# Two neighbouring tokens per partition in a gated linear attention with an MLP mixer behind it, on one core

## The chip, the cores and the metric

The kernel runs on one core of a Trainium2 chip. A core has five engines with queues of their own that meet only at semaphores: TensorE (PE, matrix products into the eight banks of PSUM), VectorE (DVE), ScalarE (ACT), GpSimd (POOL) and SyncE (SP, which here only issues transfers). Transfers run on sixteen DMA engines that all queues share. PE loads the stationary operand (PEld) apart from the product itself. The metric is the time of one execution on the device in microseconds (us), lower is better.

## What is computed

Inputs are q, k, v and f_logit, each [4 batches, 8 heads, 768 tokens, 48], and four weight matrices. Per batch and head:

```python
f = 1.0 / (1.0 + np.exp(-f_logit))
for t in range(S):
    state = f[:, :, t, :, None] * state + np.einsum('bhd,bhe->bhde', k[:, :, t], v[:, :, t])
    y[:, :, t] = np.einsum('bhd,bhde->bhe', q[:, :, t], state)
```

The heads of y are put side by side (x is [4, 768, 384]), and a mixer follows, over the tokens and then over the channels:

```python
h = np.maximum(xt @ w_tok1, 0.0) @ w_tok2          # xt: x with tokens last; 768 -> 256 -> 768
u = x + h.transpose(0, 2, 1)
out = u + np.maximum(u @ w_ch1, 0.0) @ w_ch2       # 384 -> 1536 -> 384
```

## The kernel before, in words

**The attention in chunks.** 768 tokens are six chunks of 128. Within a chunk, a running sum L of log(1 + exp(-f_logit)) over the tokens turns the gates into factors: q is multiplied by exp(-L), k by exp(+L); then y is a masked product of scores within the chunk, plus q times the state that the chunks before left. A token is a partition: `load` (lines 351 to 363) brings one chunk of q, k, v (cast to bf16 on the way, on POOL's queue) or f_logit as 1024 runs of 192 bytes.

Per batch b and chunk c, on the engines:

- `gates` (443): ACT Exp and Ln of f_logit (450, 452), DVE or POOL the low part of the split into two bf16 halves (457).
- `sums_and_turns` (504): the running sums as two bf16 products with a triangle of ones, 384 columns each (530, 531; in batch 0 also 1-column products for the chunk's totals, 528 and 529, and two chunks in one fp32 product, 519); ACT takes exp of both signs (541, 543) and, from batch 1 on, the last rows (550), one partition of which SP spreads over the partitions (556, `glast`); DVE multiplies q and k by the factors (562); eight PE transposes (579) and copies to SBUF (592, or 430 and 432). In batch 3 SP's DMA transposes do that (569).
- `attention` (461): scores in eight products of 48 rows by 128 columns, two heads in the two halves of PE's rows (476); the chunk's part of the state in eight products whose 64 output columns go to the two halves of PE's columns (492). All other products use the whole 128x128 array.
- `rest` (597): DVE masks the scores into `AmT` (616), state and its bf16 copy `state_bd` are brought up to date (625 to 640), and the outputs are four products with the state (651) and eight with the masked scores (658), copied to x_nat (fp32) and x_bf (bf16).

Batches 1 to 3 take two chunks at a time.

**The mixer** (688): tok1 is 12 products of 384 columns (693), tok2 another 12 (709), both per batch; u is turned by PE (750) in batches 0 and 1 and by SP's DMA transposes (739) in 2 and 3; ch1 is 72 products (768), with a ReLU on ACT (439) or DVE (441) into zT; ch2 is 72 products (787), DVE adds u (793) and SP stores 128 token rows of 1536 bytes (797).

**The order of the work.** Nothing is scheduled by the hardware: `Plan.best` (176) walks the long list ORDER of operation numbers (and of the engine, where an operation may go to several), gives each a time from a table of costs (SLOTS and HELD are assumed landing times of batch 0's loads) and emits all in that order; the five queues then run in order and wait at semaphores. Where PE would idle early on, `idle` (832) issues products of a constant tile (834, `steady`). In batch 0 loads arrive chunk by chunk, the two token weights behind them; the loads of later batches run ahead.

Of the kernel before, what the change touches and what calls it, by code (L numbers as in the profile page):

```python
# [20 lines left out]
TURNED = 3  # L21
ORDER = (
# [60 lines left out]
)  # L83
KEPT = 3
SPLIT = 5
SLOTS = (5110, 5800, 7500, 8450, 9600, 10400, 11400, 13000, 14400, 14800, 16700,
         18000, 19100, 19500, 20000, 20700, 21400, 23400, 24300, 25900)
HELD = (2600, 3600, 4100, 4750, 5500, 6500)


class Op:
# [162 lines left out]
def kernel(  # L254
# [140 lines left out]
    for c in range(1, NCH):  # L395
        load("kq", 0, c)
        if c + 2 < NCH:
            mark(c + 2)
            load("f", 0, c + 2, SP)
# [468 lines left out]
```

## Time and profile before

| what | value |
|---|---|
| time, two runs | 173.04 and 174.04 us, median 173.54 |
| profiled execution, first to last instruction (its span) | 170.2 us; its time beyond that is not on the page |
| PE busy | 162.9 us, 96% |
| DVE, ACT, POOL busy | 128.0, 108.2, 99.3 us |
| matmuls in the program | 1605 |
| DMA packets | 102547, of which 95264 under 512 bytes |

The page of a profile gives, for each engine, its busy time; the span in 40 slices with the busy share in tenths; the DMA queues; the chain of work that ended last, followed back; and groups of instructions by line (L768 is line 768) and form. A group's busy time counts an instant once where instructions overlap; its mean is one instruction's own latency, which for pipelined products is longer than their spacing. The spacing is read from the starts in the timeline.

### The profile page before, as it was taken

The page shows a single profiled execution, that of the slowest core. Times are in us where ns is not written, and L with a number is a line of the kernel's source. Part 1 is how long each engine was busy: PE and PEld are TensorE (multiplying, and loading weights), DVE is VectorE, ACT ScalarE, POOL GpSimd, SP SyncE. Part 2 cuts the span into 40 slices and gives each one's busy share as a digit, 9 for nine tenths or more (in the row PEclk, how much of TensorE's full clock was granted, in tenths as well). Part 3 has the DMA queues.
Part 4 walks back from the last instruction along what each step waited for, and adds up shares of the span by engine and source line. Part 5 has one row for each costly group of instructions (what it writes and reads, how often), then busy time and mean ns, then how long its engine had stood idle before and what let it go on. Part 6 is the DMA issues. An engine that isn't in the chain of part 4 may idle for free.

```text
span 170.2 us, 4181 instructions
## 1 busy us (share of the span) xinstructions
PE 162.9 (96%) x1606; PEld 102.8 (60%) x1606; DVE 128.0 (75%) x287; ACT 108.2 (64%) x256; POOL 99.3 (58%) x134
## 2 busy tenths in 40 slices
PE   6899999999999999999999999999999999999992
PEld 2356565665766576665776756665666666566661
DVE  5679995966898998899999868768884723675431
ACT  4759993598879889999999978385545320510100
POOL 7999569896499969999978869603111200000000
PEclk9999999999999999999999999999999999999999
DMA  6999999999999997999998999996920060220253
GB/s 103 141 174 149 156 192 181 212 149 201 192 167 136 161 165 75 116 155 133 182 157 49 134 251 107 144 165 115 228 100 4 0 139 0 92 96 0 78 202 139
DMA packets 102547, 22.71 MB, mean 133 GB/s; under 512 B 95264, under 2 KB 101664, under 8 KB 102528
## 3 DMA queue, kind: packets, MB, share of 16 engines
q0 software_dynamic: 79440, 13.77, 101.8%
q1 hardware_dynamic: 22560, 8.59, 22.5%
q8 instruction: 12, 0.20, 0.5%
q10 hardware_dynamic: 528, 0.10, 0.3%
q14 instruction: 7, 0.06, 0.1%
HBM read 25.17 MB, written 4.72 MB: 176 GB/s over the span
## 4 chain that ended last, share of the span: by engine, by line
PE 64%; DMA 12%; DVE 7%; ACT 6%; POOL 6%; issue 2%; SPq 1%; DVEq 0%; POOLq 0%
PE ps L768 22%; PE ps L787 22%; DMA v_sb<-in_v_dram 5%; PE ps L709 4%; POOL qk_sb L360 4%; PE ps L693 4%; DMA glast<-ends 4%; DMA out_dram<-x_nat 3%; DVE AmT L616 2%; PE ps L476 2%; PE ps L579 2%; PE ps L658 2%; POOL v_sb L360 1%; PE ps L530 1%; PE ps L651 1%
## 5 line engine op out<-in xcount | busy, mean ns | idle before, releaser
L787 PE MATMUL ps<-w_ch,zT 128*128 128x384 bf16 (+2 forms) x300 | 51.6, 320 | 0.0
L768 PE MATMUL ps<-uT,w_ch 128*128 128x384 bf16 x288 | 50.6, 326 | 0.0
L439 ACT ACTIVATE zT<-ps 128x384 bf16<-128x384 f32 x56 | 25.3, 494 | 25.3 <-PE ps L768 25.2
L768 PEld LDWEIGHTS <-w_ch 128*128 128x128 bf16 x288 | 27.7, 98 | 17.7
L787 PEld LDWEIGHTS <-zT 128*128 128x128 bf16 x300 | 27.9, 98 | 16.9
L616 DVE TENSOR_TENSOR AmT<-ps,tri_bf 128x512 bf16<-128x512 f32 x46 | 30.5, 686 | 2.5 <-PE ps L476 2.3
L441 DVE TENSOR_SCALAR zT<-ps 128x384 bf16<-128x384 f32 x40 | 21.1, 554 | 8.8 <-PE ps L768 8.8
L360 POOL DMA_DIRECT2D v_sb<-in_v_dram x24 | 22.2, 925 | 4.1 <-DMA w_ch<-in_moe_w_ch_dram 4.1
L360 POOL DMA_DIRECT2D qk_sb<-in_k_dram x24 | 22.4, 932 | 0.8 <-POOLq L852 0.8
L360 POOL DMA_DIRECT2D qk_sb<-in_q_dram x24 | 22.3, 930 | 0.0
L793 DVE TENSOR_TENSOR x_nat<-x_nat,ps 128x384 f32<-128x384 f32 (+2 forms) x25 | 13.3, 535 | 10.6 <-PE ps L787 10.2
L360 POOL DMA_DIRECT2D f_sb<-in_f_logit_dram x18 | 16.5, 943 | 0.2
L562 DVE TENSOR_TENSOR qk<-qk_sb,GG 128x768 bf16<-128x768 bf16 (+1 forms) x30 | 14.2, 475 | 2.1 <-ACT GG L543 1.0
L450 ACT ACTIVATE f_sb<-f_sb 128x384 f32<-128x384 f32 x24 | 12.5, 524 | 4.6 <-DMA f_sb<-in_f_logit_dram 4.4
L434 POOL CAST state_bd<-state 48x192 bf16<-48x192 f32 x13 | 4.5, 347 | 16.2 <-DVE state L633 14.6
L725 DVE TENSOR_TENSOR x_nat<-x_nat,ps 128x384 f32<-128x384 f32 x21 | 10.5, 550 | 3.4 <-PE ps L709 3.1
L834 PE MATMUL ps<-steady 128*128 128x512 bf16 x30 | 11.3, 483 | 1.7 <-DVE steady L375 1.7
L543 ACT ACTIVATE GG<-ps 128x384 bf16<-128x384 f32 x24 | 11.6, 489 | 2.0 <-PE ps L531 1.9
L541 ACT ACTIVATE GG<-ps 128x384 bf16<-128x384 f32 x24 | 11.7, 488 | 1.4 <-PE ps L531 1.2
L579 PE MATMUL ps<-ident,qk 128*128 128x128 bf16 x144 | 11.6, 224 | 0.0
L579 PEld LDWEIGHTS <-qk 128*128 128x128 bf16 x144 | 9.2, 100 | 2.7 <-DVE qk L562 0.7
L550 ACT ACTIVATE ends<-ps 32x384 f32<-32x384 f32 x15 | 7.0, 481 | 4.9 <-PE ps L531 4.7
(81 smaller groups left out, 234.1 us busy)
## 6 DMA issues: line engine op xcount, KB each, us to landing
out_dram<-x_nat SPq DMA_DIRECT2D x23, 192.0 KB, 3.1
f_sb<-in_f_logit_dram POOLq DMA_DIRECT2D x18, 192.0 KB, 5.4
qk_sb<-in_k_dram POOLq DMA_DIRECT2D x24, 96.0 KB, 5.1
qk_sb<-in_q_dram POOLq DMA_DIRECT2D x24, 96.0 KB, 4.9
v_sb<-in_v_dram POOLq DMA_DIRECT2D x24, 96.0 KB, 5.5
w_ch<-in_moe_w_ch_dram POOLq DMA_DIRECT2D x2, 576.0 KB, 7.5
w_ch<-in_moe_w_ch_dram POOLq DMA_DIRECT2D x1, 1152.0 KB, 10.6
f_sb<-in_f_logit_dram SPq DMA_DIRECT2D x5, 192.0 KB, 4.7
```

The source lines that it names most:

```text
L360: lambda eng=eng, into=into, of=of: eng.dma_start(out=into, in_=of),
L439: nc.scalar.activation(out_, in_, AF.Relu, bias=0.0, scale=1.0)
L441: nc.vector.tensor_scalar(out_, in_, 0.0, None, ALU.max)
L450: add(ACT, r, lambda: nc.scalar.activation(fb, fb, AF.Exp, bias=0.0, scale=-1.0), make=[key], kind=el, need=([("fb", c)] if c < 1 else []) ...
L541: add(ACT, r, lambda: nc.scalar.activation(G[i], sview(), AF.Exp, bias=0.0, scale=-1.0), make=[("G", i)], bank=p_s, kind=el)
L543: add(ACT, r, lambda: nc.scalar.activation(Gi[i], sview(), AF.Exp, bias=0.0, scale=1.0), make=[("Gi", i)], bank=p_s, kind=el)
L562: add(DVE, r, lambda n=n: nc.vector.tensor_tensor(qk[i4][:, n, :, 0:D], qk_sb[nb][:, n, :, c, :], GG[i][:, n], ALU.mult), need=[(x, nb, c) ...
L579: nc.tensor.transpose(to[:, o + hp, :], blk(src)[:, hp, :], ident)
L616: add(DVE, r, lambda half=half, made=made: nc.vector.tensor_tensor(half, made(), tb4, ALU.mult), need=["tri_bf"], make=[("AmT", i, p)], ba ...
L768: nc.tensor.matmul(banks[pm.at][:, 0:384], lhsT=w[:, kt, c0:c0 + 128], rhs=uT[:, th, :, kt, :], start=(kt == 0), stop=(kt == 2))
L787: nc.tensor.matmul(banks[pm.at][:, 0:n1 - n0], lhsT=zT[:, kt, tt * 128:(tt + 1) * 128], rhs=w_ch2[:, kt, n0:n1], start=(kt == 0), stop=(kt ...
L793: add(DVE, rank("ch2", tt), lambda un=un, pm=pm, n=n1 - n0: nc.vector.tensor_tensor(un, un, banks[pm.at][:, 0:n], ALU.add), make=[("x_nat" ...
```

## The change

One partition now holds two neighbouring tokens, and two chunks (256 tokens) are one unit: partition q of pair P holds tokens 2q and 2q+1 (index j), and the two chunks are the two halves of the partitions (index x, 64 partitions each). The loads bring 384-byte runs, 1024 of them, once per pair.

- Exp and Ln run on 768 elements at a time, with Ln in place. DVE (in batch 0 once POOL) adds the two tokens of a partition (`two`), takes a low part for batches 1 to 3 (`two_lo`), and the sums are over token pairs: two bf16 products per pair of chunks in place of four, one fp32 product in batch 0, with a triangle that is zero between the two halves. This gives the sum at each second token; the first token's is had by subtraction on DVE (`first`). ACT takes four exponentials per pair, two of them from `first`.
- The scores of a pair are 32 products of 48 rows, 64 output columns and 128 streamed columns, in the four quarters of PE's array; the state's parts 32 (16 for a lone chunk) with 64 rows, 64 output columns and 48 streamed ones, in batch 0 in two lots of 16; the products with the state 16 per pair, with 64 output columns each; those with the masked scores 32, with 64 rows each.
- In the mixer the output tile of a chunk has token 2i+j in partition 64j+i. So w_tok1 is loaded in two halves of 64 partitions, each tok2 product becomes two, one for each half of the output partitions, and the store of a tile writes through a pattern of 2 x 64 rows where it was 128 rows.
- ORDER, SLOTS, HELD and the ranks are new. In the program of after the ReLU into zT is on ACT 71 times and on DVE 25 (56 and 40 before), three of the q,k multiplications of batch 0 are on POOL, and of the 25 stores twelve stand beside the last 48 products of ch2, some of them of batches 1 and 2.

The diff, cut to its core:

```diff
-            into = dst[i][:, :, cs, :]
-            of = src[b].rearrange("h (c t) d -> t h c d", t=C)[:, :, cs, :]
+    def runs(src, b, P):
+        return src[b].rearrange("h (c q j) d -> q h c (j d)", q=C, j=2)[:, :, P, :]
...
+    for j in range(2):
+        add(POOL, 5.0, lambda j=j: nc.gpsimd.dma_start(
+            out=w_tok1[64 * j:64 * j + 64], in_=moe_w_tok1.rearrange("(kt i j) n -> j i kt n", i=64, j=2)[j]),
...
+        op.fn = lambda op=op: both(op, two[i][:, :, 0:D], fb[:, :, 0], fb[:, :, 1], ALU.add)
+        if b:
+            add(DVE, r, lambda: nc.vector.tensor_tensor(two_lo[i], two[i][:, :, 0:D], two_hi[i], ALU.subtract),
...
+            if b == 0:
+                nc.tensor.matmul(pm, lhsT=tri, rhs=two[i][:, :, 0:D], start=True, stop=True)
+            else:
+                nc.tensor.matmul(pm, lhsT=tri2, rhs=two_hi[i], start=True, stop=False)
+                nc.tensor.matmul(pm, lhsT=tri2, rhs=two_lo[i], start=False, stop=True)
...
+        add(DVE, r, lambda: nc.vector.tensor_tensor(first[i], sview(), fb[:, :, 1], ALU.subtract),
...
+        def scores(js):
             for hp in range(HP):
+                for x in range(2):
+                    for par in range(2):
+                        rows = slice(par * 64, par * 64 + D)
+                        nc.tensor.matmul(
+                            banks[p_a[js][par].at][half[x], hp * 128:(hp + 1) * 128].rearrange("p (j t) -> p j t", j=2),
+                            lhsT=qkT[s][rows, js, 4 + hp, half[x]], rhs=qkT[s][rows, :, hp, half[x]], start=True, stop=True)
...
+                            nc.tensor.matmul(dg(x)[par * 64:par * 64 + 64, hp, :], lhsT=qk[s][half[x], js, 1, h, :],
+                                             rhs=v_sb[nb][half[x], h, 2 * P + js, :],
...
+        def before(x, start):
             for hp in range(HP):
+                for j in range(2):
+                    nc.tensor.matmul(yh(x)[half[j], 2 * hp:2 * hp + 2, :], lhsT=qkT[s][:, j, hp, half[x]],
+                                     rhs=state_bd[(2 * P + x - 1) % 3][:, hp, :],
...
+                        nc.tensor.matmul(yh(x)[:, h, :], lhsT=AmT[i][half[x], js, (h % 2) * 4 + h // 2, :],
+                                         rhs=v_sb[nb][half[x], h, 2 * P + js, :],
...
-                    nc.tensor.matmul(banks[pm.at][:, 0:DM], lhsT=w_tok2[:, kt, tt * 128:(tt + 1) * 128],
+                    for j in range(2):
+                        nc.tensor.matmul(banks[pm.at][64 * j:64 * j + 64, 0:DM], lhsT=w_tok2[:, kt, tt * 128 + j:(tt + 1) * 128:2],
...
-        rows = out[b].rearrange("(tt p) n -> tt p n", p=128)
+        rows = out[b].rearrange("(tt i j) n -> tt j i n", i=64, j=2)
...
-                add(SP, rank("ch2", tt), lambda un=un, to=to: nc.sync.dma_start(out=to, in_=un),
-                    need=[("x_nat", xn, tt, n0) if end else ("x_nat", xn, tt)], kind=("fix", 350, 2000, 580))
+                add(SP, rank("ch2", tt), lambda un=un, to=to: store(to, un),
+                    need=[("x_nat", xn, tt, n0) if end else ("x_nat", xn, tt)], kind=("fix", 420, 4000 if b < 3 else 2000, 580, 0))
```

More of the change, by code (lines that the diff above doesn't have):

```diff
@@ L185, in best @@
         ports: dict = {DVE: [], POOL: []}
+        turned: list = []
         done = []
@@ L375 @@
     nc.vector.memset(steady, 1.0)
-    load_half(0, 0, SP)
-    load_half(0, 1, ACT)
-    load("f", 0, 1, SP)
-    plan.ops[-1].behind = plan.ops[-3]
+    load_half(0, SP)
+    load_half(1, ACT)
     once(ACT, lambda: nc.scalar.preload_act_table_set("natural_log_exp_and_others"), ["table"], 1280)
@@ L392 @@
+    masks = [("mask", n, x) for n in range(3) for x in range(2)]
     load("v", 0, 0)
+    mark(1)
+    load("f", 0, 1, SP)
+    load("kq", 0, 1)
+    load("v", 0, 1)
     mark(2)
     load("f", 0, 2, SP)
[L395 to L399, printed above, removed]
-        if c < NCH - 2:
-            load("v", 0, c)
-    load("v", 0, NCH - 2)
-    load_w("w_tok1", w_tok1, moe_w_tok1, 1900)
-    load("v", 0, NCH - 1)
@@ L407 @@
+    once(DVE, lambda: nc.vector.memset(ones[0:64, 0:1], 1.0), ["ones"], 60)
+    once(DVE, lambda: nc.vector.memset(ones[64:128, 1:2], 1.0), ["ones"], 60)
     for i in range(2):
-        for n, tl in (("L", L[0]), ("Llo", Llo[0])) if i == 0 else ():
-            once(DVE, lambda tl=tl: nc.vector.memset(tl[:, :, :, D:64], 0.0), [(n, i, c) for c in range(NCH)],
-                 780 if n == "L" else 400)
+        once(DVE, lambda i=i: nc.vector.memset(two[i][:, :, D:64], 0.0), [("two", i)], 200)
+        once(DVE, lambda i=i: nc.vector.memset(ends[i][:, :, D:64], 1.0), [("ends", i)], 200)
@@ L441, in relu @@
             nc.vector.tensor_scalar(out_, in_, 0.0, None, ALU.max)
-    def gates(b, c, r):
-        fb = f_sb[b % 2][:, :, c, :]
-        full = L[b % 2][:, c, :, 0:D]
-        hi = Lhi[b % 2][:, c, :, 0:D]
-        lo = Llo[b % 2][:, c, :, 0:D]
-        key, whole, rest = ("f", b % 2, c), ("L", b % 2, c), ("Llo", b % 2, c)
-        el = ("el", DM, False, 1)
-        add(ACT, r, lambda: nc.scalar.activation(fb, fb, AF.Exp, bias=0.0, scale=-1.0), make=[key], kind=el,
-            need=([("fb", c)] if c < 1 else []) + ["table"] if b == 0 else [])
-        add(ACT, r, lambda: nc.scalar.activation(full, fb, AF.Ln, bias=1.0, scale=1.0), need=[key], make=[whole], kind=el)
-        if b == 0 and c >= SPLIT:
-            return
-        on = (DVE, DVE, (DVE, POOL), POOL)[b]
-        op = add(on, r, None, need=[whole] + [key] * (b % 2), make=[rest], kind=("el", DM, False, 1.2))
-        op.fn = lambda: (nc.vector if op.engine == DVE else nc.gpsimd).tensor_tensor(lo, full, hi, ALU.subtract)
@@ L506, in sums_and_turns, with both, gates @@
-    def sums_and_turns(b, c, r):
-        i, i4, nb, g4 = c % 2, c % 4, b % NB, (b * NCH + c) % 4
-        last = c == NCH - 1
-        split = b or c < SPLIT
-        hi_c, lo_c = Lhi[b % 2][:, c], Llo[b % 2][:, c]
-        lk, rk = ("L", b % 2, c), ("Llo", b % 2, c)
+    def both(op, out_, a, b_, what):
+        (nc.vector if op.engine == DVE else nc.gpsimd).tensor_tensor(out_, a, b_, what)
+    def gates(b, P, r):
+        fb = f_sb[b % 2][:, :, 2 * P:2 * P + 2, :]
+        key, el = ("f", b % 2, P), ("el", 2 * DM, False, 1)
+        add(ACT, r, lambda: nc.scalar.activation(fb, fb, AF.Exp, bias=0.0, scale=-1.0), make=[key], kind=el,
+            need=(["fb"] if P < 1 else []) + ["table"] if b == 0 else [])
+        add(ACT, r, lambda: nc.scalar.activation(fb, fb, AF.Ln, bias=1.0, scale=1.0), make=[key], kind=el)
@@ L535, in sums_and_turns, with totals @@
+        def totals():
+            for hp in range(HP):
+                nc.tensor.matmul(banks[p_s.at][:, DM + 2 * hp:DM + 2 * hp + 2], lhsT=blk(two[i])[:, hp, :], rhs=ones,
+                                 start=True, stop=True)
+        add(PE, r, sums, need=[("two", i)] + (["tri2", ("two_lo", i)] if b else ["tri"]), bank=p_s, room=3,
+            kind=mms(*[DM] * (2 if b else 4)))
         plan.ops[-1].before.update(chains[-2:-1])
+        if b == 0:
+            add(PE, r + 1.0, totals, need=["ones", ("two", i)], bank=p_s, kind=("mm", 460))
@@ L540, in sums_and_turns @@
         el = ("el", DM, True, 1)
-        add(ACT, r, lambda: nc.scalar.activation(G[i], sview(), AF.Exp, bias=0.0, scale=-1.0),
-            make=[("G", i)], bank=p_s, kind=el)
-        add(ACT, r, lambda: nc.scalar.activation(Gi[i], sview(), AF.Exp, bias=0.0, scale=1.0),
-            make=[("Gi", i)], bank=p_s, kind=el)
-        if not last and b < 1:
+        add(DVE, r, lambda: nc.vector.tensor_tensor(first[i], sview(), fb[:, :, 1], ALU.subtract),
+            need=[("f", b % 2, P)], make=[("first", i)], bank=p_s, kind=el)
@@ L595, in sums_and_turns @@
-        return p_t if b == 0 else [p_t[0], Bank()]
-    def rest(b, c, r, p_a, p_d, dg):
-        i, i4, nb, g4 = c % 2, c % 4, b % NB, (b * NCH + c) % 4
-        last = c == NCH - 1
-        el = ("el", DM, True, 1)
-        for p in range(2):
-            half = AmT[i][:, 4 * p:4 * p + 4, :]
-            def made(p=p):
-                return banks[p_a[p].at].rearrange("s (hp t) -> s hp t", t=C)
-            if b == 0 and p == 1 and c in (3, 4):
-                add(ACT, r, lambda half=half, made=made: nc.scalar.activation(
-                    half, made(), AF.Copy, bias=0.0, scale=1.0),
-                    make=[("AmT", i, p)], bank=p_a[p], kind=("el", 512, True, 1))
-                add(POOL, r, lambda half=half: nc.gpsimd.affine_select(
-                    out=half, in_=half, compare_op=ALU.is_ge, fill=0.0, base=0,
-                    pattern=[[0, 4], [1, C]], channel_multiplier=-1),
-                    make=[("AmT", i, p)], kind=("fix", 760, 760)).before.add(loaded)
-            else:
-                add(DVE, r, lambda half=half, made=made: nc.vector.tensor_tensor(half, made(), tb4, ALU.mult),
-                    need=["tri_bf"], make=[("AmT", i, p)], bank=p_a[p], kind=("el", 512, True, 1))
-        vk = ("v", nb, c)
-        if not last:
-            gb = glast[g4].unsqueeze(2).broadcast_to((128, HP, D))
@@ new lines, in across @@
+                for x in range(2 if P < 2 else 1):
+                    nc.sync.dma_start(out=glast[g][:, x], in_=ends[i][64 * x + 63:64 * x + 64].rearrange("o par d hp -> o (par d) hp"))
+            add(SP, r, across, need=[("ends", i)], make=[("glast", g)], kind=("fix", 1000 if P < 2 else 500, 5500, 200, 0))
+        for n in (1, 0):
+            add(ACT, r, lambda n=n: nc.scalar.activation(GG[i][:, 0, n], first[i], AF.Exp, bias=0.0, scale=2.0 * n - 1.0),
+                need=[("first", i)], make=[("G", i, 0, n)], kind=("el", DM, False, 1))
@@ L623, in rest @@
             small = ("el", HP * D, True, 1)
             if b == 0:
-                add(DVE, r, lambda: nc.vector.tensor_tensor(dg(), dg(), gb, ALU.mult),
-                    need=[("glast", g4)], make=["sums"], bank=p_d, kind=small)
+                add(PE, r, lambda x=x: parts([x]), need=have, make=["sums"], bank=p_st, kind=("mm", 380))
+                add(DVE, r, lambda x=x, gb=gb: nc.vector.tensor_tensor(dg(x), dg(x), gb, ALU.mult),
+                    need=[("glast", g)], make=["sums"], bank=p_st, kind=small)
@@ L643, in rest @@
-        p_y = Bank()
-        def y():
-            return banks[p_y.at][:, 0:DM]
-        def before():
-            yh = y().rearrange("t (h e) -> t h e", e=D)
+                         need=["state" if b else "sums", ("sbd", c % 3)], make=[("sbd", c % 3, cols.start)],
+                         kind=("el", HP * D, b == 0, 1), bank=None if b else p_st)
+                op.fn = lambda op=op, rows=rows, cols=cols, x=x, c=c: copy_on(
+                    op.engine, state_bd[c % 3][rows, :, cols], state[rows] if b else dg(x)[rows])
@@ L665, in outs @@
         def outs():
-            if c > 0:
-                before()
+            if P:
+                before(0, True)
             within()
-        past = [("qkT", i4, 0), ("sbd", j), ("sbd", j, 0), ("sbd", j, D)] if c > 0 else []
-        add(PE, r, outs, need=[*past, ("AmT", i, 0), ("AmT", i, 1), vk], bank=p_y,
-            kind=mms(*([96] * 4 if c else []), *[48] * 8))
-        if b == 0 and c >= KEPT:
-            kept[c] = p_y
-        for tl, key in ((x_bf[b % 2], ("x_bf", b % 2, c)), (x_nat[b % 3], ("x_nat", b % 3, c)))[
-                :1 if b == 0 and c >= KEPT else 2]:
-            if b == 0 and tl is x_bf[0] and c < KEPT:
-                continue
-            op = add((ACT, DVE), r, None, make=[key], bank=p_y, kind=el)
-            op.fn = lambda op=op, tl=tl: copy_on(op.engine, tl[:, c, :], y())
@@ L681, in rest, with past @@
-        if b == 0 and c < KEPT:
-            late = add((POOL, ACT, DVE), r, None, need=[("x_nat", 0, c)], make=[("x_bf", 0, c)], kind=("el", DM, False, 1))
-            late.fn = lambda: copy_on(late.engine, x_bf[0][:, c, :], x_nat[0][:, c, :])
+        def past(x):
+            return [("qkT", s, 0), ("qkT", s, 1)] + [("sbd", (2 * P + x - 1) % 3, *n) for n in ((), (0,), (D,))]
+        ready = (past(0) if P else []) + [("AmT", i, js, par) for js in range(2) for par in range(2)] + [("v", nb, P)]
@@ new lines, in attention @@
+        lead = add(PE, r, lambda: None, need=ready, bank=p_y[0], kind=("mm", 1), room=2)
+        lead = add(PE, r, outs, need=ready, bank=p_y[1], kind=("mm", (170 if P else 0) + 560), tail_of=lead)
+        plan.maker[p_y[0]] = lead
+        add(PE, r, lambda: before(1, False), need=past(1), bank=p_y[1], kind=mms(*[96] * 4))
+        for x in range(2):
+            c = 2 * P + x
+            y = lambda x=x: banks[p_y[x].at][:, 0:DM]
+            if b == 0 and c >= KEPT:
+                kept[c] = p_y[x]
+            for tl, key in ((x_bf[b % 2], ("x_bf", b % 2, c)), (x_nat[b % 3], ("x_nat", b % 3, c)))[
+                    :1 if b == 0 and c >= KEPT else 2]:
+                if b == 0 and tl is x_bf[0] and c < KEPT:
+                    continue
+                op = add((ACT, DVE), r, None, make=[key], bank=p_y[x], kind=("el", DM, True, 1))
+                op.fn = lambda op=op, tl=tl, c=c, y=y: copy_on(op.engine, tl[:, c, :], y())
+            if b == 0 and c < KEPT:
+                late = add((POOL, ACT, DVE), r, None, need=[("x_nat", 0, c)], make=[("x_bf", 0, c)], kind=("el", DM, False, 1))
+                late.fn = lambda late=late, c=c: copy_on(late.engine, x_bf[0][:, c, :], x_nat[0][:, c, :])
@@ L686, with store @@
     kept, chains = {}, []
+    def store(to, un):
+        nc.sync.dma_start(out=to, in_=un)
     def mixer(b, rank):
```

373 lines of the change are left out of this document (178 added, 195 removed), and 116 rows, old and new, of the table ORDER.

## The prediction

> **What bounds the kernel now.** I read the busy times first, then the slices and queues, then stretches of the span.
>
> ```profile
> span 170.2 us, 4181 instructions
> PE 162.9 (96%) x1606; PEld 102.8 (60%) x1606; DVE 128.0 (75%) x287; ACT 108.2 (64%) x256; POOL 99.3 (58%) x134
> DMA  6999999999999997999998999996920060220253
> ...
> q0 software_dynamic: 79440, 13.77, 101.8%
> ```
>
> PE is busy nearly throughout; the DMA engines are full for three quarters of the span. To see which of them ends a stretch:
>
> ```profile
> core 0: us, PE busy (x) PEld busy (x) DVE busy (x) ACT busy (x) POOL busy (x), PEclk, DMA share, GB/s
> 14.00:25.00 11.00, 10.49 (x167) 6.90 (x167) 10.66 (x27) 10.28 (x28) 7.55 (x11) 1.00 2.02 166
> ...
> 0.00:25.20 25.20, 22.54 (x262) 12.60 (x263) 20.35 (x64) 18.65 (x46) 20.41 (x34) 1.00 1.84 152
> 32.00:125.00 93.00, 92.48 (x996) 60.59 (x995) 80.45 (x169) 76.49 (x182) 69.94 (x88) 1.00 1.60 153
> 125.00:167.00 42.00, 41.59 (x292) 25.55 (x288) 22.21 (x45) 9.01 (x19) 2.18 (x6) 1.00 0.21 69
> ```
>
> From 32 us to 167 PE idles 0.93 of 135 us at granted clock 1.00. There the time is PE's own work, and whatever a product costs more is paid in full. In the head, up to ch1, PE partly runs constant products (L834); what holds it there the chain shows:
>
> ```profile
> 11.54 8.27 DMA v_sb<-in_v_dram
> 19.85 0.31 PE ps L492 x8
> ...
> 24.61 0.75 PE ps L834 x3
> 25.37 0.65 PE ps L693 x4
> ...
> 32.22 7.80 PE ps L768 x48
> ```
>
> The load of v for chunk 3 takes 8.27 us to land and PE's queue stands behind it at 19.85. But from 14 to 25 DVE is busy 10.66 of 11 us and ACT 10.28: faster loads alone would meet full engines.
>
> **The change, part by part.** *Head.* A pair's load moves the bytes of two loads in half the runs, so v of the last pair lands well before 25 us. DVE's work of batch 0 falls: five low parts and twelve multiplications become two `two`, three `first` and three wider multiplications; ACT's twelve Exp/Ln of 384 become six of 768.
>
> ```profile
> L457 DVE TENSOR_TENSOR Llo<-L 128x384 bf16<-128x384 f32 x9 | 4.9, 556 | 1.2 <-ACT L L452 1.2
> L562 DVE TENSOR_TENSOR qk<-qk_sb,GG 128x384 bf16<-128x384 bf16 x12 | 4.2, 353 | 0.4 <-ACT GG L541 0.4
> L562 DVE TENSOR_TENSOR qk<-qk_sb,GG 128x768 bf16<-128x768 bf16 x18 | 9.9, 556 | 1.7 <-ACT GG L543 1.0 <-ACT GG L541 0.6
> L450 ACT ACTIVATE f_sb<-f_sb 128x384 f32<-128x384 f32 x24 | 12.5, 524 | 4.6 <-DMA f_sb<-in_f_logit_dram 4.4
> L608 ACT ACTIVATE AmT<-ps 128x512 bf16<-128x512 f32 x2 | 1.2, 586 | 0.0
> L550 ACT ACTIVATE ends<-ps 32x384 f32<-32x384 f32 x15 | 7.0, 481 | 4.9 <-PE ps L531 4.7
> L439 ACT ACTIVATE zT<-ps 128x384 bf16<-128x384 f32 x56 | 25.3, 494 | 25.3 <-PE ps L768 25.2
> L441 DVE TENSOR_SCALAR zT<-ps 128x384 bf16<-128x384 f32 x40 | 21.1, 554 | 8.8 <-PE ps L768 8.8
> L616 DVE TENSOR_TENSOR AmT<-ps,tri_bf 128x512 bf16<-128x512 f32 x46 | 30.5, 686 | 2.5 <-PE ps L476 2.3
> ```
>
> DVE: 5x0.556 + 12x0.353 = 7.0 us against 5x0.556 + 3x0.556 = 4.4 us, so 2.6 us less; the ten masks (0.686 each) stay. ACT saves about as much: 512 elements take 0.586 us and 384 take 0.494, 0.07 for each 100 more, so that 768 come to 0.524 + 0.28 = 0.80, and six of those against twelve of 0.524, twice, for Exp and for Ln, are 3.0 us less. If DVE sets the head, 2.6 us are won. Bounds: nothing (the first scores now wait for two tokens' gates, and the lone fp32 sum runs before them) and 5 us (all of the waiting for v goes). I take 2.6, since DVE's 97% is the nearest row.
>
> *PE after the head.* The spacing of products, from the starts:
>
> ```profile
> 43.85 1.63 PE L768 MATMUL ps<-uT,w_ch 128*128 128x384 bf16 x9
> 45.41 0.62 PE L476 MATMUL ps<-qkT 48*128 48x128 bf16 x16
> 45.97 0.43 PE L492 MATMUL ps<-v_sb,qk 128*64 128x48 bf16 x16
> 46.33 2.77 PE L787 MATMUL ps<-w_ch,zT 128*128 128x384 bf16 x16
> ...
> 50.13 0.33 PE L530 MATMUL ps<-f_sb,tri_bf 128*128 128x384 bf16 x1
> 50.30 0.32 PE L531 MATMUL ps<-Llo,tri_bf 128*128 128x384 bf16 x1
> 50.46 0.33 PE L651 MATMUL ps<-state_bd,qkT 128*128 128x96 bf16 x4
> 50.63 0.36 PE L658 MATMUL ps<-v_sb,AmT 128*128 128x48 bf16 x8
> 50.83 1.46 PE L787 MATMUL ps<-w_ch,zT 128*128 128x384 bf16 x8
> ```
>
> A product of 384 columns costs 7.80/48 = 0.1625 us. Nine of them are 1.46, but 1.56 pass before the scores start: 0.10 us where PE goes from the whole array to halves. The same 0.10 lies between scores and parts and behind the parts: 16 scores take 0.56 where eight pairs at the pace of 128 columns (0.056) would take 0.45; 16 parts take 0.36. So two halves do run side by side, and every change of the array's partition costs about 0.095 us. In PE's program, behind the last tok1 of batch 0, I count 27 such changes before and 71 after: scores and parts now share one partition (quarters), but the products with the state, those with the masked scores and tok2 have left the whole array. 44 more x 0.095 = **+4.2 us**.
>
> The rest of that stretch, in batches 1 to 3: sums, 18 products fewer x 0.1625 = **-2.9**. Scores: twice as many, four abreast where two were: 0 (if only two run abreast, 9 pairs x 0.45 = +4.0). Parts: from 15x8 at 0.016 each = 1.9 us to 48 groups of four at about 0.039 plus 24 pairs at 0.032 = 2.6: **+0.7** (a pair's 0.032 and an allowance, my estimate, of 0.0035 for each further start). Masked scores: 144 at 0.025 = 3.6 become 144 pairs at 0.025 and the allowance = 4.1: **+0.5** (alone +3.6). Products with the state: 60 at 0.042 become 60 pairs at 0.046: **+0.2** (alone +2.5). tok2: 48 become 48 pairs: **+0.2** (alone 48x0.1625 = +7.8). Where I write "alone", the second half runs after the first; rows 476 and 492 show pairs, so I take the lower end. Sum of the stretch: **+2.8 us**.
>
> DVE and ACT do not take over as the bound. DVE gains 32 sums and differences (11 `two`, 9 `two_lo`, 12 `first`, 17.8 us at 0.556), loses 15 low parts (8.3), 15 ReLUs (8.3) and about 2.4 of multiplications: -1.2. ACT gains 15 ReLUs (+7.4), and loses 24x0.524 - 12x0.80 = 3.0 us on Exp and as much on Ln, and 2.9 on six exponentials of last rows (0.481 each). POOL issues half as many transfers; it was off the path. SP's fifteen spreads and ten transposes stay; its transposes stand behind stores as before.
>
> *Tail.* The last product now ends a full tile, where it ended 96 columns:
>
> ```profile
> L793 DVE TENSOR_TENSOR x_nat<-x_nat,ps 128x384 f32<-128x384 f32 x23 | 12.6, 550 | 10.1 <-PE ps L787 9.7
> L793 DVE TENSOR_TENSOR x_nat<-x_nat,ps 128x96 f32<-128x96 f32 x1 | 0.3, 255 | 0.1
> ...
> 145.30:145.90 0.60, 0.60 (x6) 0.36 (x4) 0.60 (x3) 0.46 (x1) 0.00 (x0) 1.00 0.98 369
> ...
> out_dram<-x_nat SPq DMA_DIRECT2D x12, 192.0 KB, 1.9
> out_dram<-x_nat SPq DMA_DIRECT2D x1, 48.0 KB, 1.6
> ```
>
> 0.550 - 0.255 + 1.9 - 1.6 = **+0.6 us**. A store keeps its bytes and its 1536-byte rows, so by the nearest row (192 KB in 1.9) it costs what it did; twelve of them beside the last 48 products are 12 x 0.5 us of data in 7.6 us. The other bound is in the first rival.
>
> **Sum:** 170.2 - 2.6 + 2.8 + 0.6 = 171.0 us of span. The median of the runs, 173.54, is 3.3 above the profiled span, so 174.3 us: no change within 2%, which is about what a measurement of this kernel can tell.
>
> **Rivals.** *1. The stores narrow to two DMA engines; slower.* The store's pattern in memory was 128 rows and is now 2 x 64; every transfer before has 128 partitions or rows outermost, so no row shows what a 2 does. In the window of stores alone (145.30 to 145.90) all 16 engines are 0.98 busy and move 369 GB/s, 23.5 GB/s each; a tile of 196.6 KB is 0.52 us. If an outer 2 leaves two engines, it is 196.6/2/23.5 = 4.2 us. In mid-kernel PE need not wait long. But the order puts ten whole tiles and two parts (3.1 and 1.1 us) beside the last 48 products: 46 us of data that start about 6 us before PE ends. The end then comes about 41 us behind PE instead of about 3: 174.3 + 38 = 212 us. It decides from the point where a store takes over 0.6 us, twelve in 7.6. For it: the outermost count is the only thing about the stores that changes. Against it: the rows, bytes and partitions are the same.
>
> The Trainium skill speaks for it: "DMA: Bandwidth & Descriptors", in "Rules for kernel authors", says that the number of engines is set by the slowest dimension that is not 1 of both patterns, and that an outer dimension of c below 16 confines a transfer to at most c engines. By that rule each store goes on two engines and the sum would be the 212 us of this rival. No run here shows the rule, since nothing in this trace has a small outer dimension.
>
> *2. The head was bound by the loads; faster.* All 5 us go and first scores are no later: 170.2 - 5 + 2.8 + 0.6 + 3.3 = 171.9, still within 2%; with half of the partition changes where PE waits anyway, 169.8. For it: the chain's 8.27 us on v. Against it: DVE and ACT at 97 and 93% in the same stretch.
>
> *3. The narrow products do not run abreast.* +4.0, +3.6, +2.5, +7.8 and about +1.5 for parts, 19 us: 193 us. Against it: rows 476 and 492, two abreast both by rows and by columns.
>
> *4. PE waits for DVE between 45 and 105 us.* A pair's chain has three more DVE steps (0.556 each) ahead of its exponentials, and the q,k buffers are two where they were four. Nine pairs x 0.5 us: 179 us. For it:
>
> ```profile
> 65.00:85.00 20.00, 19.87 (x206) 13.27 (x204) 18.95 (x43) 19.41 (x49) 19.95 (x25) 1.00 1.76 140
> ```
>
> DVE and ACT are nearly full there. Against it: PE has ch1 and ch2 of the batch before to fill with, and hardly idles.
>
> **How the numbers follow.** Forecast 0.40, rival 1 0.38 (the rows bear out neither end, the pattern changes), rival 2 0.06, rival 3 0.04, rival 4 0.12. The forecast's own range is 171 (head won up to 5) to 177 (half of what "alone" adds to scores and tok2 less its cover). For eight in ten the range has to reach into rival 1: 171 to 214. Faster by over 2% (under 170.1): rival 2 and a little of the forecast, 0.08. Within 2%: 0.38. Slower (over 177.0): rivals 1, 3, 4, 0.54.
>
> **What would show each step.** Head: ch1 of batch 0 starts near 29.5 us where it started at 32.1. PE: last product of 384 columns before a change spaced 0.26, tok2 pairs 0.166 apart, PE's end about 0.2 us later than 167. Tail: stores at the end landing in 1.9 us; landings of 5 us and more, growing one behind the other, with a DMA share of 2/16 after PE's end, would be rival 1. Wrong it would be, too, if PE idled over 1 us after 32 us.

## The result, and the profile after

The changed kernel takes 221.93 us (221.68 and 222.17) where the kernel before takes 173.54: 1.282 times as long, 95% interval 1.267 to 1.297. Its profiled execution took 222.17 us, of which the span is 220.5. Where an experiment's executions differ in the granted clock of the head (e5: spans of 178.5 to 184.5 us at mean clocks of 0.98 to 0.95), the profiled execution's own span and stretches are compared, not the median.

From the page of the kernel after: the counts, and the span in 40 slices of 5.5 us each.

```profile
span 220.5 us, 5344 instructions
PE 169.0 (77%) x2231; PEld 105.9 (48%) x2234; DVE 126.4 (57%) x277; ACT 107.3 (49%) x235; POOL 63.2 (29%) x89
...
PE   6659999999999999999992999999999980000000
...
PEclk9965999999999999999999699999999998555555
DMA  7999979999999208197929544115411111111110
GB/s 109 187 182 193 207 128 140 230 214 213 222 227 218 22 1 72 40 151 88 64 66 107 122 57 103 53 55 72 87 34 53 33 45 50 52 50 50 50 50 37
```

PE has nothing to do in the last seven slices, and through them the DMA engines move some 50 GB/s. The other places that differ from before are slices 2 to 4, where PE is less busy and then its clock is low, and slice 22. The same in stretches (columns as in the windows of before; the DMA share adds up the times of packets, and passes 1 where they overlap), the last in a second answer:

```profile
0.00:25.20 25.20, 18.63 (x181) 12.15 (x184) 13.73 (x44) 12.06 (x22) 16.85 (x25) 0.80 1.40 173
...
120.00:150.00 30.00, 28.41 (x388) 16.98 (x389) 18.31 (x38) 13.15 (x30) 2.76 (x8) 0.94 0.33 74
...
182.00:215.00 33.00, 0.00 (x0) 0.00 (x0) 0.00 (x0) 0.00 (x0) 0.00 (x0) 0.56 0.13 50
```

Behind PE's end the DMA share is 0.13, that is 2 of 16 engines, at 25 GB/s each. In the timeline of SP of the kernel after (start, duration, engine, line):

```profile
103.03 1.17 SPq L675 DMA_DIRECT2D out_dram<-x_nat  x2
106.69 3.77 SPq L518 DMA_TRANSPOSE qkT<-qk  x1
110.50 0.51 SPq L675 DMA_DIRECT2D out_dram<-x_nat  x1
...
114.55 4.44 SPq L729 DMA_TRANSPOSE uT<-u_bf  x2
...
159.45 49.78 SPq L675 DMA_DIRECT2D out_dram<-x_nat  x15
```

The last fifteen stores begin at 159.45, and the end is at 220.5: 61 us for fourteen tiles' bytes, 4.4 us a tile with the waits for ch2 in it. In the chain of the kernel after (start, duration), the first transposed u behind the stores:

```profile
114.55 7.00 DMA uT<-u_bf
```

In the timeline of PE of the kernel after, with the idle time and its releaser in brackets:

```profile
10.43 0.62 PE L528 MATMUL ps<-ident,qk 128*128 128x128 bf16 x8 [1.14 <-DVE qk L443]
...
14.02 1.04 PE L528 MATMUL ps<-ident,qk 128*128 128x128 bf16 x8 [2.54 <-DVE qk L443]
...
15.54 1.65 PE L468 MATMUL ps<-two,tri 128*128 128x384 f32 x2
16.98 1.71 PE L475 MATMUL ps<-ones,two 128*128 128x2 f32 x8
...
38.56 1.62 PE L758 MATMUL ps<-uT,w_ch 128*128 128x384 bf16 x9
...
121.59 1.14 PE L758 MATMUL ps<-uT,w_ch 128*128 128x384 bf16 x3 [4.29 <-DMA uT<-u_bf]
...
179.68 1.30 PE L777 MATMUL ps<-w_ch,zT 128*128 128x384 bf16 x7
```

ch1 begins at 38.56 (32.06 before), and the last product ends at 180.98 (166.83). So the 50.3 us more of span are:

| stretch | before | after | more |
|---|---|---|---|
| to the first product of ch1 | 32.06 | 38.56 | 6.5 |
| from there to PE's last end | 134.77 | 142.42 | 7.7 |
| behind PE's end | 3.4 | 39.5 | 36.1 |

Of the 7.7, 4.3 are the wait for the transposed u of batch 2 (the product that waits at 121.59 is the 145th of ch1, the first of the third of its batches 0 to 3; the expectation of e1 calls it batch 3). Its transfer stands behind stores: it is issued at 114.55 and takes 7.00 us to land, where in e2 below, with the same order, it is issued at 110.53 and takes 3.2. About 1.8 are the clock of 0.94 in the stretch around it (0.06 x 30 us), and about 1.5 are left for the change of PE's products.

### The profile page after: what moved, and what is told of

Read it like the earlier page. It is cut to its first block, busy times and chain, and to the rows that moved or that the text cites. A ratio compares the mean times of both kernels' runs of the same rounds, so it can differ in the third digit from the quotient of the medians.

```text
span 220.5 us, 5344 instructions
## 1 busy us (share of the span) xinstructions
PE 169.0 (77%) x2231; PEld 105.9 (48%) x2234; DVE 126.4 (57%) x277; ACT 107.3 (49%) x235; POOL 63.2 (29%) x89
## 4 chain that ended last, share of the span: by engine, by line
PE 70%; DMA 6%; DVE 2%; POOL 1%; ACT 1%; issue 1%; SPq 0%; POOLq 0%; DVEq 0%; ACTq 0%
PE ps L758 22%; PE ps L777 20%; PE ps L528 4%; PE ps L682 4%; PE ps L699 4%; DMA f_sb<-in_f_logit_dram 3%; DMA uT<-u_bf 3%; PE ps L554 3%; PE ps L638 3%; PE ps L630 3%; PE ps L571 2%; PE ps L818 1%; PE ps L468 1%; PE ps L475 1%; POOL qk_sb L353 1%
## 5 line engine op out<-in xcount | busy, mean ns | idle before, releaser
L596 DVE TENSOR_TENSOR AmT<-ps,mask 128x512 bf16<-128x512 f32 x46 | 30.2, 682 | 3.4 <-PE ps L554 3.4
L508 ACT ACTIVATE GG<-first 128x384 bf16<-128x384 f32 x24 | 11.7, 520 | 10.4 <-DVE first L488 10.2
L491 ACT ACTIVATE GG<-ps 128x384 bf16<-128x384 f32 x24 | 11.3, 492 | 6.7 <-PE ps L475 5.1
L443 DVE TENSOR_TENSOR qk<-qk_sb,GG 128x768 bf16<-128x768 bf16 x21 | 11.9, 568 | 4.4 <-ACT GG L508 2.6
L353 POOL DMA_DIRECT2D v_sb<-in_v_dram x12 | 10.7, 889 | 5.4 <-DMA w_ch<-in_moe_w_ch_dram 4.0
L448 ACT ACTIVATE f_sb<-f_sb 128x768 f32<-128x768 f32 x12 | 10.1, 843 | 4.2 <-DMA f_sb<-in_f_logit_dram 4.1
L431 DVE COPY qkT<-ps 128x1024 bf16<-128x1024 bf16 x16 | 10.8, 683 | 1.1 <-PE ps L528 1.1
L353 POOL DMA_DIRECT2D qk_sb<-in_k_dram x12 | 10.9, 905 | 1.8 <-issue 0.9
L353 POOL DMA_DIRECT2D qk_sb<-in_q_dram x12 | 10.8, 897 | 0.7 <-DMA qk_sb<-in_q_dram 0.3
L682 PE MATMUL ps<-x_bf,w_tok 128*128 128x384 bf16 x48 | 10.7, 327 | 0.0
```

What stands on the lines that cost most here:

```text
L353: lambda eng=eng, into=held(dst[i], P), of=runs(src, b, P): eng.dma_start(out=into, in_=of),
L443: (nc.vector if op.engine == DVE else nc.gpsimd).tensor_tensor(out_, a, b_, what)
L491: add(ACT, r, lambda n=n: nc.scalar.activation(GG[i][:, 1, n], sview(), AF.Exp, bias=0.0, scale=2.0 * n - 1.0), make=[("G", i, 1, n)], ban ...
L508: add(ACT, r, lambda n=n: nc.scalar.activation(GG[i][:, 0, n], first[i], AF.Exp, bias=0.0, scale=2.0 * n - 1.0), need=[("first", i)], make ...
L596: add(DVE, r, lambda into=into, made=made, m4=m4: nc.vector.tensor_tensor(into, made(), m4, ALU.mult), need=masks, make=[("AmT", i, js, pa ...
L682: add(PE, rank("tok1", rt), lambda rt=rt, kt=kt, pm=pm: nc.tensor.matmul(banks[pm.at][:, 0:DM], lhsT=w_tok1[:, kt, rt * 128:(rt + 1) * 128 ...
```

## The experiments

**The theory** for the largest part: a store whose pattern has an outermost 2 runs on two DMA engines. Its rivals: rows that lie 3072 bytes apart are slow to write, or SP's issuing is the limit.

### e1 and e2: the same stores with 64 or 128 rows outermost

```diff
 e1 -        nc.sync.dma_start(out=to, in_=un)
 e1 +        for j in range(2):
 e1 +            nc.sync.dma_start(out=to[j], in_=un[64 * j:64 * j + 64])
 e2 -        rows = out[b].rearrange("(tt i j) n -> tt j i n", i=64, j=2)
 e2 +        rows = out[b].rearrange("(tt p) n -> tt p n", p=128)
```

> The changed kernel with each store issued as two transfers of 64 rows, one for each of the two tokens, so that 64 rows are outermost; rows, strides, bytes and order stay. Theory (an outermost 2 leaves two DMA engines): each tile lands in under 4 us, the DMA share beside the last products rises from 2/16 to well over it, the tail behind PE's last product shrinks from 39 to 3 or 4 us (-35.6), and the 4.3 us hole before ch1 of batch 3 goes with what it costs in clock (1.8): 222 - 42 = 180 us (178 to 183). Rival (the alternate rows, 3072 bytes apart, make the writes slow): nothing changes, 222 us. Rival (SyncE's issuing is the limit): twice the issues, 222 or more.

> The changed kernel with the 128 rows of a tile stored one behind the other, so 128 rows are outermost and neighbouring; the rows of a tile land in another order than the reference has. Theory (two engines): as the kernel with the split stores, within 1.5 us of it, about 180. Rival (alternate rows slow): also 180, which with the split kernel at 222 would tell the two apart.

e2 took 180.46 us (one execution), as the theory said. e1 took 186.25 (185.89 to 188.55; 1.085 times its before, 1.079 to 1.091): 36 us less than the changed kernel, so the distance between rows costs nothing that shows, but 5 us more than expected. In e2 (span 178.8) PE's stretch is 136.3 us and 3.6 us lie behind it; no wait for u above 0.4 us is left. The DMA issues of e2, with the last column the median us to landing:

```profile
out_dram<-x_nat SPq DMA_DIRECT2D x23, 192.0 KB, 2.1
```

In e1 each half lands in 2.2 us, and most of what is missing is in the timeline of SP, here of an execution of 188.55 us:

```profile
168.99 15.25 SPq L676 DMA_DIRECT2D out_dram<-x_nat  x24
```

24 halves at 0.635 us of issuing each end at 184.2, 7.6 us behind PE's end at 176.6, and the end of the span is 10.2 us behind it, 6.6 more than in e2. Another 1.5 us of this execution are in the head: the granted clock is 0.51 from 10.6 to 27.9 us, and ch1 begins at 40.49 where it begins at 38.97 in e2. So issuing is a limit too, once the transfers are wide; it is not what held the changed kernel.

### e3, e4 and e11: only the store's pattern changed, in the kernel before

```diff
-        rows = out[b].rearrange("(tt p) n -> tt p n", p=128)
+        rows = out[b].rearrange("(tt i j) n -> tt j i n", i=64, j=2)      # e3; e4: i=16, j=8; e11: i=32, j=4
```

> The kernel before with only its stores changed to the 2 x 64 pattern (rows of a tile land in another order than the reference has). Theory (two engines, 3.95 us a tile in place of 0.52): fourteen stores from 144.5 us on, worth 13 tiles, need 51 us, and the transposes of u for batch 3 come some 4 us late behind six stores: 173.5 + about 29 = 200 to 206 us. If the stores matter only together with the new order, or not at all: 173 to 175 us.

> The kernel before with its stores in an 8 x 16 pattern (rows of a tile land in another order than the reference has). Theory (as many engines as the outermost count): a tile is 1.05 us of data on eight engines, the fourteen stores fit beside the products, and only the last lands later: 173.5 to 176 us, a share of about 0.5 in windows full of stores. Rival (a pattern of three dimensions or alternate rows is slow by itself): near the kernel with 2 x 64, 200 us.

> The kernel before with its stores in a 4 x 32 pattern (rows of a tile land in another order than the reference has). Theory (as many engines as the outermost count): 196.6 KB / (4 x 25 GB/s) = 1.97 us a tile, fourteen stores from about 147 us on, worth 13 tiles, need 25.6 us and cannot end before 173, some 4 us behind the kernel with 8 x 16; 179 to 184 us, with a DMA share of 0.25 behind PE's last product. Rival (small outer counts share one slow path whatever their size): near the 228 of 2 x 64.

Measured, in one execution each: 227.9 us with 2, 193.0 with 4 and 177.7 with 8 outermost. The order is the theory's; but the times are 22, 9 and 1.7 us above the upper ends expected (the kernel before took 171.2 to 175.9 us beside them, so the 1.7 say little). The engines in use are read from windows in which only stores move (the last two columns are the DMA share and GB/s), in e3, e11 and e4:

```profile
195.00:220.00 25.00, 0.00 (x0) 0.00 (x0) 0.00 (x0) 0.00 (x0) 0.00 (x0) 0.52 0.13 50
```

```profile
177.00:186.00 9.00, 0.00 (x0) 0.00 (x0) 0.00 (x0) 0.00 (x0) 0.00 (x0) 0.61 0.27 98
```

```profile
169.30:173.00 3.70, 0.00 (x0) 0.00 (x0) 0.01 (x1) 0.00 (x0) 0.00 (x0) 0.91 0.53 189
```

2, 4 and 8 sixteenths, at 24 to 25 GB/s an engine; with 128 outermost the window of before had 0.98 and 369. The Trainium skill says so ("DMA: Bandwidth & Descriptors", "Rules for kernel authors": an outer dimension of c below 16 confines a transfer to at most c engines), and the runs agree in all three counts. In e1 the rows lie as far apart as in the changed kernel, so the distance is not the cause.

What the expectation of e3 missed is in its list of waits (engine, line, releaser: us in total, times, longest) and in PE's timeline:

```profile
DVE x_nat L432 <- DMA out_dram<-x_nat: 17.0, 1, 17.0
```

```profile
113.24 0.60 PE L476 MATMUL ps<-qkT 48*128 48x128 bf16 x8 [4.13 <-DMA qkT<-qk]
...
139.50 0.48 PE L693 MATMUL ps<-x_bf,w_tok 128*128 128x384 bf16 x1 [5.92 <-ACT x_bf L430]
...
151.52 0.50 PE L651 MATMUL ps<-state_bd,qkT 128*128 128x96 bf16 x4 [9.30 <-ACT x_bf L430]
```

The first of the three gaps is a transpose of q and k that stands behind a store in SP's queue. The two others come from a buffer: batch 3 writes its x where batch 0 had its own, and narrow stores are still reading that. ScalarE waits 6.4 us for one of them and VectorE 17.0, and PE for what they copy. e11 has two such gaps of PE, of 3.3 us each. A slow store thus costs at the end, and it holds a buffer in the middle. What the expectation did name, u of batch 3 late by 4 us, did not come: ch1 of that batch starts at 169.42 with no wait shown.

### e5: half of the late stores issued by ScalarE

```diff
+            (nc.scalar if j and late else nc.sync).dma_start(out=to[j], in_=un[64 * j:64 * j + 64])
```

> The kernel with the split stores, and for the stores beside the last products the second half of each issued by ScalarE, whose ReLUs are done by then. Theory (the split kernel's tail of 10 us is SyncE issuing 24 halves at 0.64 us each, not their data): the last landing comes 3 or 4 us behind PE's last product, 186.2 - 5.5 = 180.7 us (180 to 182), as with rows one behind the other. Rival (transfers of 64 partitions are slow by themselves): 185 to 186.

Four executions took 180.23, 180.45, 183.94 and 186.23 us. The profiled one, of 180.45, has 4.2 us behind PE's last end: the theory's number. This kernel is the base of what follows.

### e6 to e8: the head

In the kernel after ScalarE takes things in this order (its timeline):

```profile
11.71 0.84 ACT L448 ACTIVATE f_sb<-f_sb 128x768 f32<-128x768 f32 x1 [2.38 <-DMA f_sb<-in_f_logit_dram]
12.45 0.92 ACT L508 ACTIVATE GG<-first 128x384 bf16<-128x384 f32 x2
```

The second pair's Exp stands ahead of the first pair's exponentials, and waits for its load. Behind it PE idles 2.54 us ahead of the transposes at 14.02; meanwhile the clock falls, and the fp32 sums at 15.54 take 1.65 us, where those at 6.71 took 0.91. Is it the clock or the load? e6 puts 15 more constant products where PE idles, e7 takes away the mark for which the second load of the gates waits, and e8 does both:

```diff
 e6, e8  +                n += {1: 5, 2: 10}.get(sum(o.kind[0] == "fill" for o in done), 0)
 e7, e8       mark(1)
         +    plan.ops[-1].fn = lambda: None
```

> As e5, with 15 more constant products in two places of PE's queue (5 ahead of the first transposes, 10 ahead of the second), where PE idles 1.1 and 2.5 us; nothing else. Theory (the head is long because PE's idling lowers its granted clock to 0.5 from 12 to 22 us, in which it is busy throughout with fp32 sums): clock 1.00 there, ch1 of batch 0 starts some 4.5 us sooner, 176 us (175 to 178). Rival (the head is a chain of waits for gates and loads): ch1 starts within 1 us of e5's, 180 to 182.

> As e5, with the gates' second load (768 tokens' second pair, 384 KB) issued at once, where it waits for a mark that GpSimd sets behind the first q, k, v loads; nothing else. Theory (the second pair's Exp stands ahead of the first pair's exponentials on ScalarE and waits 2.4 us for that load): the gap of 2.5 us ahead of the second transposes goes, the clock holds longer, ch1 starts 2.5 to 5 us sooner, 176 to 178.5 us. Rival (the first k and q come later by as much, since the loads share the engines): no gain, 180 to 182.

> As e5 with both, the early load and the 15 constant products. Theory clock: where the gap is closed already, the products cost up to 3 us of PE in front of the work and give the clock: 175 to 178, and no better than the better of the two alone by more than 1.5 us.

e6 took 179.53 us (179.02 to 181.63), e7 177.47 and e8 178.95 (one execution each). ch1 began at 38.16 us in e5, 36.11 in e6, 35.10 in e7 and 35.84 in e8. Windows of e5 and of e7:

```profile
10.00:15.00 5.00, 2.47 (x34) 1.79 (x34) 2.97 (x7) 2.81 (x6) 1.82 (x3) 0.72 1.65 184
15.00:20.00 5.00, 5.00 (x68) 4.00 (x63) 2.84 (x9) 3.38 (x6) 2.67 (x4) 0.50 1.77 182
```

```profile
10.00:15.00 5.00, 4.33 (x92) 3.43 (x92) 4.58 (x14) 3.02 (x6) 3.01 (x5) 1.00 1.67 183
15.00:20.00 5.00, 3.74 (x64) 2.60 (x58) 3.74 (x9) 3.62 (x9) 3.94 (x4) 1.00 1.67 190
```

The clock is worth 2.0 us, not the 4.5 that I expected (e6 has it at 1.00 through the head, and pays for it with the time of 15 products), and the load 3.1 with the clock in it. The two do not add up: with the early load the long gap is gone and in e7 the clock holds, and e8 gains nothing over e7. That the long gap is what lowers the clock is not shown. In the kernel after, the clock is at 0.50 from 12.2 to 22.4 us, and at 12.2 only 0.7 of the 2.54 us had passed; in e1 it is at 0.51 from 10.6 to 27.9, with a gap of 1.14 us just ahead; in e12, the kernel of e7 once more, it is at 0.57 from 8.0 to 12.0. The Trainium skill ("TensorE: Matmul & The Clock Gate", "Why this matters for your kernels") warns of idle gaps above about 3 us; in the heads here no gap was that long, and the clock fell all the same.

### e9, and e12 to e15: what is left of the head

```diff
 e9          - add((DVE, POOL) if b == 0 else DVE, r, None, need=[(x, nb, P) for x in "qk"] ...
 e9          + add((DVE, DVE) if b == 0 else DVE, r, None, need=[(x, nb, P) for x in "qk"] ...
 e13, e15    - lhsT=blk(two[i])[:, hp, :], rhs=ones
 e13, e15    + lhsT=(the upper bf16 halves of two[i])[:, hp], rhs=(ones in bf16)
 e14, e15         mark(2)
             +    plan.ops[-1].fn = lambda: None
```

> As e7, with the three q,k multiplications of batch 0 that were on GpSimd (1.65 us each, one behind the other from 17.3 to 22.1 us) on VectorE (0.55 each); nothing else. Theory (what is left of the longer head is a chain through GpSimd: gates, then these multiplications, then the transposes that wait for them): first product of ch1 1 to 2.5 us sooner than e7's 35.1, 175 to 176.5 us. Rival (VectorE or the fp32 sums hold the head): ch1 within 0.5 us of e7's, 177 to 178. Rival (more work on VectorE, busy 3.7 to 4.6 of 5 us there, delays masks): slower.

> The kernel of e7 once more, timed beside the next ones: 177 to 178 us if its head clock holds at 1.00 as in the first look; up to 182 in executions in which it does not.

> As e12, with the eight 2-column fp32 products of a pair's totals as bf16 products of the upper halves alone (leaves out the lower half of each gate sum in the totals of batch 0). Theory (the fp32 totals, 0.8 us a pair, stand between the sums and the exponentials that wait for them): the wait for them shrinks by 0.6 us at each of three pairs, ch1 starts 0.6 to 1.8 us sooner than 35.1. Rival (loads hold the head): ch1 within 0.4 us.

> As e12, with the third pair's gates also loaded at once (SyncE issues all three at the start). Theory (e7's chain begins with that load, issued at 7.15 us and landed at 14.38): its Exp starts 1 us or more sooner, the third pair's sums too (17.4 in e7), ch1 1 to 2 us sooner, 175.5 to 176.5 us. Rival (q, k and v of the first pair then land 1.2 us later and hold the first transposes): no gain, or 1 us worse.

> As e12 with both. If waits of one chain are taken away, the gains of e13 and e14 add, ch1 by 32.5 to 33.5 us and about 175 us; if they are covers of one another or GpSimd's multiplications hold the end of the head, no better than the better one.

| run | time, us | span profiled | ch1 starts | granted clock, 15 to 25 us |
|---|---|---|---|---|
| e9 | 178.72 (178.02 to 179.33) | 176.9 | 36.17 | 0.93, 0.73 |
| e12 | 178.94 (177.54 to 179.34) | 175.8 | 35.35 | 1.00, 1.00 |
| e13 | 179.28 | 177.6 | 37.17 | 0.88, 0.50 |
| e14 | 177.26 (176.20 to 178.34) | 174.5 | 34.10 | 1.00, 1.00 |
| e15 | 176.20 | 174.5 | 34.34 | 1.00, 1.00 |

In e14 ch1 starts sooner by 1.25 us than in e12, whose clock was down before 15 us, and by 1.0 than in e7, whose clock held. That is what its theory said of the head, but the time, 177.26, lies above the 175.5 to 176.5 expected (the profiled execution took 176.20). e9 missed, and so did e13, whose PE idled 2.7 us from 14.7 on and then ran at half clock for five; with the clock down in both, neither tells what its change is worth. In e15 the clock held, and ch1 starts no sooner than in e14: no gain of the totals is shown on top of it. e9's other executions, at mean clocks of 0.99 to 1.00, have spans of 176.3 to 177.6, and those of e12 are 175.8 to 177.6: GpSimd's multiplications are not shown to be the chain either. At a clock of 1.00 and with both loads early (e14), 2.0 us of longer head stay unexplained.

Even so mended, e14 takes 1.032 times as long as the kernel before (1.019 to 1.044).

### e10: tok2 over the whole array

```diff
-                    for j in range(2):
-                        nc.tensor.matmul(banks[pm.at][64 * j:64 * j + 64, 0:DM], lhsT=w_tok2[:, kt, tt * 128 + j:(tt + 1) * 128:2],
+                    nc.tensor.matmul(banks[pm.at][:, 0:DM], lhsT=w_tok2[:, kt, tt * 128:(tt + 1) * 128],
```

> As e7, with each pair of tok2's half products as one product over the whole array (its output rows lie in another token order than the reference has). Theory (a change of the array's partition costs 0.094 us): in batches 1 to 3 tok2 has 7 entries and 7 exits, and the pairs 0.166 a piece, so PE's stretch from ch1 of batch 0 to its last product is shorter by 14 x 0.094 = 1.3, and a few tenths of pairs: 136.3 becomes 134.8 us (134.4 to 135.2). Rival (the changes are hidden or cost nothing): 136 to 136.5.

PE's stretch from ch1 to its last end is 134.0 us (e7: 136.3), 2.3 less, where 1.1 to 1.9 less were expected; the time is 175.37 (one execution each). In e7, before and behind a burst of tok2 (timeline of PE):

```profile
70.45 0.81 PE L780 MATMUL ps<-w_ch,zT 128*128 128x384 bf16 x4
71.19 2.22 PE L702 MATMUL ps<-h1T,w_tok 128*64 128x384 bf16 x24
73.34 0.82 PE L780 MATMUL ps<-w_ch,zT 128*128 128x384 bf16 x4
```

Four products of 384 columns take 0.74 us ahead of the narrow ones, where 4 x 0.1625 is 0.65: 0.09 for entering. 24 half products take 2.15, where twelve whole ones take 1.95: 0.10 for leaving and 0.10 for twelve pairs. Over the seven bursts of batches 1 to 3 that is 14 x 0.094 = 1.3 us and 0.2 to 0.3 of pairs, so the changes of partition do cost what the theory said. 0.4 more of e10's gain is a gap of PE for u ahead of 115.55 us that e10 does not have; that is luck. About 0.3 are left, most of them closer spacings in the transposes of q and k, which the edit does not touch.

## Why the prediction was wrong, step by step

**The step that failed is the store's.** "A store keeps its bytes and its 1536-byte rows, so by the nearest row (192 KB in 1.9) it costs what it did." The row is nearest in bytes and in run length, and those did stay. What changed is the outermost count of the pattern, and the runs show that this sets the number of engines: 3.9 us of data a tile (196.6 KB at 50 GB/s) where there were 0.5. The term of the tail, +0.6, measured +36.1. The text had the mechanism, its price and its point of decision (0.6 us a store) in the first rival, and gave it 0.38 against 0.40. Its sum of 41 us behind PE's end stands beside 39.5 measured. (Not quite every transfer of before has 128 outermost: the fifteen spreads of 2 KB, line 556, read a single partition. They are too small to show a rate.)

**"In mid-kernel PE need not wait long"** was wrong by 6 us: 4.3 of waiting for u of batch 2, whose transposes are issued 4.0 us later and land 3.8 us more slowly than in e2, and 1.8 of clock beside it. In e3, with the order of before, it was 19 us of gaps.

**The head: -2.6 forecast, +6.5 measured.** The sum held VectorE, 97% busy there, to be the bound, and its work did fall, if by less than 2.6: up to the first product of ch1 it is busy 23.88 us against 25.30. But it was not what the head waited for: of the first 25.2 us VectorE is busy 13.73, against 20.35. Shown are 2.0 us for the clock, 3.1 for the second gate load with the clock in it, 1.0 to 1.25 for the third's, and 2.0 are open. The likely reason, not shown by itself, is that with half as many loads of twice the size, and gates of a pair where they were of a chunk, each step of the chain is longer and fewer steps overlap. Rival 2 (the load of v as the bound) falls with it: the last v of batch 0 lands earlier than before (21.7 us against 25.3), and ch1 starts later; the loads that e7 and e14 show to count are those of the gates. This error and the mid-kernel one are why 222 lies above the rival's 212, and out of the range.

**PE's stretch: +2.8 forecast, +1.5 measured** (e2, 136.3 against 134.8). The mechanism is as the text had it: a change of the array's partition costs 0.094 us where 0.095 was reckoned, and e10 takes 14 of them away. Too dear were the parts: 32 of them take 0.25 us, 0.0078 each, where a group of four at 0.039 made it 0.0098 and a pair at 0.032 more. The sums measured -3.1 (forecast -2.9). The terms as printed add up to 2.9, not 2.8.

**Rivals 3 and 4.** 32 scores take 0.47 us where the parts follow them with no change of partition (e7, 44.76 to 45.23), and sixteen of double width took 0.56 with a change, 0.10, in it: they do run four abreast, and rival 3 is out. Behind the start of ch1 of batch 0, e7 has one gap of PE above 0.1 us, 0.37 for u; VectorE does not hold PE, and rival 4 is out.

**The signs to look for** named the stores' landings, a share of 2/16 and an end long behind PE's, and that is what the profile shows. The range's upper end, 214, took the rival's time but not its error: the head's bound on that side was that nothing is won, and a longer head was thought of only as the wait for two tokens' gates.

**Two readings of the profile of before** were loose. The DMA engines stand at 0.9 or more in 25 of the 40 slices, which is less than three quarters of the span. And of the 3.3 us put on top of the span, 1.7 is what the kernels here take beyond their span; the rest is spread between executions of the kernel before.

## What to carry to other kernels

When a transfer's pattern is rewritten, look at its outermost count before its bytes and runs: with 2, 4 and 8 on the memory side of a store it was the number of DMA engines, and a tile that took 0.5 us of data took 0.5 x 16/c. Split such a transfer by its small dimension into several whose partitions are outermost, and count what the queue pays for issuing them (0.6 us each here). And before a head is made of fewer, larger steps, follow its chain: relieving an engine that is 97% busy need not shorten it.

## What the hardware showed that was not expected

- The engines used go with the outermost count: shares of 0.13, 0.27 and 0.53 for 2, 4 and 8, each engine at 24 to 25 GB/s.
- Narrow stores of one queue do not add up: in windows with nothing else, those of the last fifteen move 50 GB/s together at a share of 0.13. That they all use the same two engines would explain it, but the profile does not name the engines.
- The granted clock of PE fell to 0.5 at 12.2 us in the kernel after, behind a gap of 1.14 us and 0.7 us into another, and stayed there until 22.4, 10.2 us in which PE was busy for 8.04. From 9 us on, with gaps of 1.3 us at most, it held in e7 and fell in e9.
- A change between the whole array and its halves costs about 0.094 us going in and 0.10 coming out (tok2 in e7).
